# RWKV attention beside a mixture of experts: from tile 10 on a round takes two tiles

## The chip, the core and the metric

The kernel runs on one core of a Trainium2 chip. The time is in microseconds (us) of the device, from one execution of the whole program; the median of three runs is used. The engines are TensorE (PE; its weight loads have a row of their own, PEld), VectorE (DVE), ScalarE (ACT), GpSimd (POOL) and SyncE (SP, which only issues transfers). In the code they are `T`, `V`, `S_`, `G` and `Q`.

## The reference

Attention is a linear recurrence over 768 steps for 4 batches of 8 heads of 48 columns; its output, 3072 tokens of 384 columns, goes through 8 experts whose weights come from a gate that is normalized in turn over rows and columns.

```python
for t in range(S):
    cur = einsum('bhd,bhe->bhde', u[None] * kt, vt)
    y[:, :, t] = einsum('bhd,bhde->bhe', rt, state + cur)
    state = w[None, :, :, None] * state + einsum('bhd,bhe->bhde', kt, vt)
...
logits = x @ w_gate
P = exp(logits - logits.max())
for _ in range(8):
    P /= P.sum(1, keepdims=True) + 1e-09
    P /= P.sum(0, keepdims=True) + 1e-09
    P *= N / E
for e in range(E):
    out += P[:, e:e + 1] * (maximum(x @ w1[e], 0.0) @ w2[e])
```

## The kernel before

**Tiles.** The tokens are 24 tiles of 128 (`NTT`), six to a batch. Attention is done tile by tile in a chunked form. For tile `tt`: `prep_k` (VectorE) scales k into `kp`; r is loaded turned by blocks (`load_blocks`), transposed in blocks by `turn_r` (VectorE, into `rp`) and scaled by `scale_r` (GpSimd, into `rT`); `stage_b` turns k on TensorE (`pkT`) and ScalarE copies it to `kT`; `stage_c` makes the scores (`pA`, 32 matmuls of 64 rows and 64 columns), which VectorE copies through a mask into `at`; `state` makes k's products with v (`pu`), to which VectorE adds the state so far and which GpSimd multiplies by the decay (`sd`); `spread` (ScalarE) lays the state out as `S` for the next tile; `stage_d` sums y in PSUM (`py`: 16 matmuls with `S`, 32 with `at`); `bonus_dot` and `bonus` make the term of u (`rk`, `dg`; GpSimd and VectorE), and `finish` (VectorE) adds it: x. `sum_x`, `scale_x` and `low_x` split x into two half-precision parts (`xsc`) and issue the DMA that transposes it into `hbx`; `stage_f` multiplies it by the gate's weights (`px`) and ScalarE copies the result to `lparts`. A tile whose number is 5, 11, 17 or 23 needs no `state`.

**Units.** Meanwhile expert 0 is computed for groups of three tiles. A unit is a piece of it on TensorE: g1 (`ph`, 9 matmuls, then a relu on ScalarE and the low half `hb` on VectorE) or g2 (`po`, 12 matmuls, then ScalarE copies it to `stg` and SyncE stores it). Units stand in a list, 8 g1 and 3 g2 for the first group, then g1 g2 g1 g2 g1 g2 g1 over and over; `work(n)` takes the next n. Units left over run after the attention.

**Side steps.** Three lists of steps prepare token combinations for the later experts: rebuilds on VectorE (`ws<-hbx`), 17 additions on GpSimd (`ws<-ws`), casts on ScalarE and low parts on VectorE (both `xv`). A cast comes three steps after the last addition that it reads. `prepare()` takes one step, if the tiles that its list needs are there.

**Order.** Every instruction goes to its engine's queue in the order in which the code makes it (`InOrder`), each engine executes its queue in that order, and semaphores between engines follow from the data. So the order of the calls in a round is the order of all queues. Buffers go round: `ps1` has two banks for `ph`, `ps2` two for `po` and `px`, `ps3` four for everything of the attention, and the loaded tiles of k and r three each, of v five. Rounds 0 to 9 and 25, 26 are `open_round`; rounds 10 to 24 are `packed_round(i)`: one unit, two units, `prepare` two or three times, the gate product of tile i - 4, the turn of k of tile i + 1, the scores of i, y of i - 1, the state of i, `prepare` twice. The helper that keeps the order records all instructions under one line, L30, so the profile is read by the names of tiles.

After the attention the gate is normalized and the other seven experts run until the end; the change does not touch that part.

Of the kernel before, what the change touches and what calls it, by code (L numbers as in the profile page):

```python
# [8 lines left out]
F32 = mybir.dt.float32  # L9
# [24 lines left out]
def rwkv_sinkhorn_moe(  # L34
# [37 lines left out]
    TX0 = 12  # L72
    PACKED = 10
    GX = 4
    NWP = 4
# [313 lines left out]
    ss_ = [ac.tile([P, NPAIR, 2, D], F32, name=f"S{i}") for i in range(2)]  # L389
    sd_ = [ac.tile([P, NPAIR, D], F32, name=f"sd{i}") for i in range(2)]  # L390
    for t_ in rp_[:1] + kp_[:1] + rp_[1:] + kp_[1:]:
# [84 lines left out]
    def scale_r(tt):  # L476
        rT = at2.tile([P, NPAIR, P], F32, tag="rT", name=f"rT_{tt}", bufs=3)
        G.tensor_tensor(rT, rp_[tt % 2].rearrange("p (a j) d -> p a (j d)", j=2), tab, op=ALU.mult)
        st.setdefault(tt, {})["rT"] = rT
# [7 lines left out]
    def prep_k(tt):  # L487
        V.tensor_tensor(kp_[tt % 3][:, :, :D], loads[tt]["k"], kt4, op=ALU.mult)

# [35 lines left out]
    def stage_b(tt):  # L525
        d = st.setdefault(tt, {})
        for nm, src in (("rT", rp_[tt % 2]), ("kT", kp_[tt % 3]))[tt >= TX0 :]:
            pt = ps3.tile([P, NPAIR, P], F32, tag="pa", name=f"p{nm}_{tt}")
            sv = src.rearrange("p (a j) d -> p a (j d)", j=2)
            for p_ in range(NPAIR):  # L530
                T.transpose(pt[:, p_, :], sv[:, p_, :], ident)
            dst = at2.tile([P, NPAIR, P], F32, tag=nm, name=f"{nm}_{tt}", bufs=3 if nm == "rT" else 2)
            S_.copy(dst, pt)
            d[nm] = dst
# [23 lines left out]
    def state(tt):  # L558
        c = tt % NCHB
        if c < NCHB - 1:  # L560
            vn = loads[tt]["v"]
            kp = kp_[tt % 3].rearrange("p (a j) d -> p a (j d)", j=2)

            pu = ps3.tile([P, NPAIR, D], F32, tag="pa", name=f"pu_{tt}")
            for p_ in range(NPAIR):
                for j in range(2):
                    T.matmul(
                        pu[j * HP : (j + 1) * HP, p_, :], kp[:, p_, j * HP : (j + 1) * HP],
                        vn[:, 2 * p_ + j, :], start=True, stop=True,
                    )  # L570
            sd = sd_[tt % 2]
            if c == 0:
                V.tensor_tensor(sd, pu, wcb, op=ALU.mult)
            else:
                V.tensor_tensor(sd, pu, sd_[(tt - 1) % 2], op=ALU.add)
                G.tensor_tensor(sd, sd, wcb, op=ALU.mult)

    def spread(tt):
        if tt % NCHB < NCHB - 1:
            sn = ss_[tt % 2]  # L580
            for j in range(2):
                rows = slice(j * HP, (j + 1) * HP)
                S_.copy(sn[rows, :, j, :], sd_[tt % 2][rows])
            st.setdefault(tt + 1, {})["S"] = sn
# [223 lines left out]
    dot_u(0)  # L808
    def packed_round(i):
        if i + 2 < NTT:  # L810
            load_round(i)
        if TX0 <= i + 1 < NTT:
            scale_r(i + 1)
        if i + 2 < NTT:
            prep_k(i + 2)
        if i + 1 < NTT:
            bonus_dot(i + 1)
        if i < NTT:
            bonus(i)
        sum_x(i - 2)  # L820
        if i < NTT:
            spread(i - 1)
        held[0] = True
        work(1)
        held[0] = False
        scale_x(i - 2)
        emitted[0] = i - 1
        form_lows()
        if i + 2 < NTT:
            turn_r(i + 2)  # L830
        low_x(i - 2)
        work(2)
        for _ in range(n_steps(i, 1)):
            prepare()
        stage_f(i - 4, ps2.tile([P, TB], F32, tag="po", name=f"px_{i}"))
        if i + 1 < NTT:
            stage_b(i + 1)
        if i < NTT:
            stage_c(i, lambda: None)
        stage_d(i - 1)  # L840
        finish(i - 1)
        if i < NTT:
            state(i)
        for _ in range(n_steps(i, 2)):
            prepare()
        if i + 4 < NTT:
            load_blocks(i + 4)

# [89 lines left out]

    for i in range(NTT + 3):
        if PACKED <= i <= NTT:  # L940
            packed_round(i)
        else:
            open_round(i)
        if i == NTT + 2:
            stage_f(i - 3, ps2.tile([P, TB], F32, tag="po", name=f"px_{i + 1}"))
        done = i - 2
        if 0 <= done < NTT and done % TH == TH - 1:
            po_ = done // TH
            if po_ == 0:
                units += [g1_unit(0, fc, W) for fc in range(FC)]  # L950
                units += [g2_half(0, t, 0, W) for t in range(TH)]
                pend = [(0, t, 1) for t in range(TH)]
            for j in range(2 if po_ else 0):
                g1 = [g1_unit(po_, fc, W) for fc in range(j * FHC, (j + 1) * FHC)]
                g2 = [g2_half(*a, W) for a in pend]
                units += merged(g1, g2)
                pend = [(po_, t, j) for t in range(TH)]
    assert not side and not wsteps
# [565 lines left out]
```

## Time and profile before

| | |
|---|---|
| median of 3 runs | 1510.43 us (1509.54 to 1510.84) |
| profiled execution | 1511.74 us, of which the span from first to last instruction is 1510.2 us |
| granted clock of TensorE | 1.00 |
| busy over the span | PE 99%, DVE 66%, ACT 46%, POOL 37% |
| rounds 10 to 26 | about 76 to 217 us of the span |

Busy time of an engine is the union of its instructions. A matmul row's duration contains the way through the array, so that successive matmuls overlap: the cost of a group on TensorE is the distance from its start to the start of the next group. The name in `out<-in` says which tile an instruction writes and reads, with buffer numbers left out. What stands in square brackets is the engine's idle time just ahead of the row and what ended it; "issue" means that nothing in the profile was waited for.

### The profile page before, as it was taken

Reading aid. Unit: us, or ns where it says so; the run is one execution under the profiler, and the core shown is the slowest. Engines: PE = TensorE matmul, PEld = TensorE weight load, DVE = VectorE, ACT = ScalarE, POOL = GpSimd, SP = SyncE. Lnnn points to the kernel's source line nnn. Section 1 sums busy time; section 2 is a strip of 40 time slices with the busy share of each in tenths; the row PEclk is TensorE's granted clock in tenths of the full one; section 3 lists DMA queues with packets and bytes.
Section 4 is the critical chain, followed back from the end, with each engine's and each line's share of the span. In section 5 each row is a group of like instructions: output and inputs, shape, how many; then the busy total and the mean of one; then the engine's idle time right before and its main releaser. Section 6 shows DMA issues by size and latency. Waiting matters only on the chain.

```text
span 1510.2 us, 26058 instructions
## 1 busy us (share of the span) xinstructions
PE 1498.7 (99%) x10228; PEld 848.4 (56%) x10228; DVE 1002.8 (66%) x1647; ACT 693.8 (46%) x1289; POOL 562.8 (37%) x667
## 2 busy tenths in 40 slices
PE   8999999999999999999999999999999999999998
PEld 6777766555555555555555555555555555555555
DVE  7888859575666666666666666656566666666563
ACT  7644545244443544445454544445353544445320
POOL 8677845200124243342425243342424233242200
PEclk9999999999999999999999999999999999999999
DMA  9777541212155566766666566655454455555433
GB/s 189 160 175 164 125 112 55 79 47 95 62 105 75 76 126 89 130 80 124 93 108 100 84 126 93 116 61 96 60 100 54 60 95 61 95 62 98 57 97 129
DMA packets 193639, 147.70 MB, mean 98 GB/s; under 512 B 110306, under 2 KB 187748, under 8 KB 193508
## 3 DMA queue, kind: packets, MB, share of 16 engines
q0 software_dynamic: 44928, 61.36, 33.0%
q1 hardware_dynamic: 148370, 84.60, 20.9%
q8 instruction: 82, 1.34, 0.4%
q14 instruction: 49, 0.40, 0.1%
q10 hardware_dynamic: 210, 0.00, 0.0%
HBM read 59.92 MB, written 80.23 MB: 93 GB/s over the span
## 4 chain that ended last, share of the span: by engine, by line
PE 96%; DVE 3%; DMA 0%; issue 0%; ACT 0%; DVEq 0%; ACTq 0%
PE po L30 49%; PE bZ L30 12%; PE bY L30 12%; PE ph L30 5%; PE bA L30 5%; PE bB L30 5%; PE py L30 3%; PE bC L30 2%; PE pA L30 1%; PE pkT L30 1%; PE pu L30 1%; DVE hb L30 0%; DMA hbx<-xsc 0%; DVE wms L30 0%; DVE xv L30 0%
## 5 line engine op out<-in xcount | busy, mean ns | idle before, releaser
L30 PE MATMUL po<-ws,hbx 128*128 128x384 f16 x3360 | 736.8, 326 | 0.0
L30 POOL DMA_DIRECT2D accd<-stg x288 | 249.8, 867 | 695.7 <-ACT stg L30 671.4
L30 PEld LDWEIGHTS <-hbx 128*128 128x128 f16 x3504 | 335.3, 98 | 294.2 <-issue 0.6
L30 PEld LDWEIGHTS <-ws 128*128 128x128 f16 x3096 | 301.7, 98 | 247.5 <-issue 2.0
L30 ACT ACTIVATE hbx<-tb 128x512 f16<-128x512 f32 x224 | 141.1, 630 | 450.5 <-DVE tb L30 450.5
L30 PE MATMUL po<-ws,hb 128*128 128x384 f16 x1248 | 323.1, 326 | 0.0
L30 DVE TENSOR_TENSOR tb<-bY,tb 128x512 f32<-128x512 f32 x168 | 116.2, 691 | 195.3 <-PE bY L30 195.2
L30 ACT ACTIVATE stg<-po,pe 128x384 f32<-128x384 f32 x312 | 179.2, 574 | 121.2 <-PE po L30 93.2
L30 PE MATMUL bZ<-xv,ws 128*128 128x512 f16 x840 | 227.0, 379 | 0.9 <-DVE tb L30 0.9
L30 PE MATMUL bY<-xv,ws 128*128 128x512 f16 x840 | 227.0, 379 | 0.0
L30 DVE TENSOR_TENSOR tb<-bZ,tb 128x512 f32<-128x512 f32 x168 | 115.5, 688 | 134.8 <-PE bZ L30 134.6
L30 PEld LDWEIGHTS <-hb 128*128 128x128 f16 x1248 | 121.4, 98 | 93.9 <-issue 0.2
L30 POOL TENSOR_TENSOR ucb<-rawb 128x256 f32<-128x256 f32 x84 | 75.5, 950 | 117.2 <-DMA rawb<-in_moe_w_dram 117.2
L30 DVE TENSOR_TENSOR tb<-bB,tb 128x512 f32<-128x512 f32 x112 | 77.4, 691 | 49.1 <-PE bB L30 47.2
L30 PE MATMUL ph<-hbx,ws 128*128 128x384 f16 x576 | 103.9, 326 | 2.3 <-DMA hbx<-xsc 1.4
L30 DVE SCALAR_TENSOR_TENSOR hb<-tb,hbx 128x512 f16<-128x512 f32 x112 | 77.2, 689 | 24.6 <-ACT hbx L30 19.5
L30 PE MATMUL bA<-xv,ws 128*128 128x512 f16 x336 | 90.8, 379 | 0.0
L30 PE MATMUL bB<-xv,ws 128*128 128x512 f16 x336 | 90.8, 379 | 0.0
L30 DVE SCALAR_TENSOR_TENSOR hbx<-tb,hbx 128x512 f16<-128x512 f32 x112 | 77.8, 695 | 14.7 <-ACT hbx L30 10.4
L30 ACT COPY tb<-bZ 128x512 f32<-128x512 f32 x56 | 32.7, 585 | 65.6 <-PE bZ L30 65.5
L30 DVE SCALAR_TENSOR_TENSOR hb<-ph,hb 128x384 f16<-128x384 f32 x64 | 35.1, 550 | 26.0 <-ACT hb L30 25.8
L30 DVE TENSOR_REDUCE wms<-rawb 128x1 f32<-128x768 f32 x56 | 51.8, 944 | 0.0
(177 smaller groups left out, 1464.8 us busy)
## 6 DMA issues: line engine op xcount, KB each, us to landing
accd<-stg POOLq DMA_DIRECT2D x288, 192.0 KB, 3.6
rawb<-in_moe_w_dram SPq DMA_DIRECT2D x28, 768.0 KB, 7.3
e0d<-stg SPq DMA_DIRECT2D x48, 192.0 KB, 2.1
hb<-e0d SPq DMA_DIRECT2D x48, 192.0 KB, 3.6
vn<-in_v_dram SPq DMA_DIRECT2D x24, 192.0 KB, 3.3
hbx<-in_r_dram SPq DMA_DIRECT2D x48, 96.0 KB, 2.5
accd<-stg SPq DMA_DIRECT2D x24, 192.0 KB, 1.8
accd<-hb POOLq DMA_DIRECT2D x24, 192.0 KB, 4.8
```

The costliest lines, as they stand in the source:

```text
L30: return lambda *a, **k: self.tc.keep_in_program_order(f(*a, **k))
```

## The change

From tile 10 on a new `double_round(a)` takes tiles a and a + 1. It first runs five or six units, each with some vector work between: the splits of x of the two tiles whose y came last, the scaling of k and r of the new tiles, side steps, and behind the fourth or fifth unit the gate products of the two tiles before those, one after the other. Then come, on TensorE: turns of k of both tiles, state's products of both, y of the two tiles before, scores of both. At its end four more side steps. Nine double rounds and a short end replace rounds 10 to 26. The gate's two tiles, r's homes (`rhome`, four in turn, one of them a part of `kp`), k's (`khome`, two in turn) and the decayed state's (three) are named by hand; loads of k, r and v from tile 14 on are issued in the double round.

```diff
@@ -71,6 +71,7 @@
     NSUM = 4
     TX0 = 12
     PACKED = 10
+    NFIRST = PACKED + 4
     GX = 4
     NWP = 4
 
@@ -387,7 +388,16 @@
     at_ = [ac.tile([P, H, C], F32, name=f"at{i}") for i in range(2)]
 
     ss_ = [ac.tile([P, NPAIR, 2, D], F32, name=f"S{i}") for i in range(2)]
-    sd_ = [ac.tile([P, NPAIR, D], F32, name=f"sd{i}") for i in range(2)]
+    sd_ = [ac.tile([P, NPAIR, D], F32, name=f"sd{i}") for i in range(3)]
+    rt_ = [ac.tile([P, NPAIR, P], F32, name=f"rT{i}") for i in range(3)]
+    rt_.append(kp_[2].rearrange("p (a j) d -> p a (j d)", j=2))
+
+    def rhome(tt):
+        return rt_[tt % 3] if tt < TX0 else rt_[(0, 3, 1, 2)[(tt - TX0) % 4]]
+
+    def khome(tt):
+        return kp_[tt % 3] if tt < TX0 else kp_[tt % 2]
+
     for t_ in rp_[:1] + kp_[:1] + rp_[1:] + kp_[1:]:
         G.memset(t_[:, :, D:], 0.0)
     fill(at_[0].rearrange("p h c -> p (h c)"))
@@ -474,7 +484,7 @@
         V.transpose(rp_[tt % 2].rearrange("p (a j) (q g) -> p a g (j q)", j=2, g=GX), x_)
 
     def scale_r(tt):
-        rT = at2.tile([P, NPAIR, P], F32, tag="rT", name=f"rT_{tt}", bufs=3)
+        rT = rhome(tt)
         G.tensor_tensor(rT, rp_[tt % 2].rearrange("p (a j) d -> p a (j d)", j=2), tab, op=ALU.mult)
         st.setdefault(tt, {})["rT"] = rT
 
@@ -485,7 +495,7 @@
         G.tensor_tensor(rp_[tt % 2][:, :, :D], loads[tt]["r"], rt4, op=ALU.mult)
 
     def prep_k(tt):
-        V.tensor_tensor(kp_[tt % 3][:, :, :D], loads[tt]["k"], kt4, op=ALU.mult)
+        V.tensor_tensor(khome(tt)[:, :, :D], loads[tt]["k"], kt4, op=ALU.mult)
 
     def prep_first():
         for j, (nm, dst) in enumerate((("r", rp_[0]), ("k", kp_[0]))):
@@ -524,12 +534,12 @@
 
     def stage_b(tt):
         d = st.setdefault(tt, {})
-        for nm, src in (("rT", rp_[tt % 2]), ("kT", kp_[tt % 3]))[tt >= TX0 :]:
+        for nm, src in (("rT", rp_[tt % 2]), ("kT", khome(tt)))[tt >= TX0 :]:
             pt = ps3.tile([P, NPAIR, P], F32, tag="pa", name=f"p{nm}_{tt}")
             sv = src.rearrange("p (a j) d -> p a (j d)", j=2)
             for p_ in range(NPAIR):
                 T.transpose(pt[:, p_, :], sv[:, p_, :], ident)
-            dst = at2.tile([P, NPAIR, P], F32, tag=nm, name=f"{nm}_{tt}", bufs=3 if nm == "rT" else 2)
+            dst = rhome(tt) if nm == "rT" else at2.tile([P, NPAIR, P], F32, tag=nm, name=f"{nm}_{tt}")
             S_.copy(dst, pt)
             d[nm] = dst
 
@@ -559,7 +569,7 @@
         c = tt % NCHB
         if c < NCHB - 1:
             vn = loads[tt]["v"]
-            kp = kp_[tt % 3].rearrange("p (a j) d -> p a (j d)", j=2)
+            kp = khome(tt).rearrange("p (a j) d -> p a (j d)", j=2)
 
             pu = ps3.tile([P, NPAIR, D], F32, tag="pa", name=f"pu_{tt}")
             for p_ in range(NPAIR):
@@ -568,11 +578,11 @@
                         pu[j * HP : (j + 1) * HP, p_, :], kp[:, p_, j * HP : (j + 1) * HP],
                         vn[:, 2 * p_ + j, :], start=True, stop=True,
                     )
-            sd = sd_[tt % 2]
+            sd = sd_[tt % 3]
             if c == 0:
                 V.tensor_tensor(sd, pu, wcb, op=ALU.mult)
             else:
-                V.tensor_tensor(sd, pu, sd_[(tt - 1) % 2], op=ALU.add)
+                V.tensor_tensor(sd, pu, sd_[(tt - 1) % 3], op=ALU.add)
                 G.tensor_tensor(sd, sd, wcb, op=ALU.mult)
 
     def spread(tt):
@@ -580,7 +590,7 @@
             sn = ss_[tt % 2]
             for j in range(2):
                 rows = slice(j * HP, (j + 1) * HP)
-                S_.copy(sn[rows, :, j, :], sd_[tt % 2][rows])
+                S_.copy(sn[rows, :, j, :], sd_[tt % 3][rows])
             st.setdefault(tt + 1, {})["S"] = sn
 
     def stage_d(tt):
@@ -806,45 +816,89 @@
     prep_r(2)
     spread_u()
     dot_u(0)
-    def packed_round(i):
-        if i + 2 < NTT:
-            load_round(i)
-        if TX0 <= i + 1 < NTT:
-            scale_r(i + 1)
-        if i + 2 < NTT:
-            prep_k(i + 2)
-        if i + 1 < NTT:
-            bonus_dot(i + 1)
-        if i < NTT:
-            bonus(i)
-        sum_x(i - 2)
-        if i < NTT:
-            spread(i - 1)
-        held[0] = True
+    def px_bank(tt):
+        return ps2.tile([P, TB], F32, tag="po", name=f"px_{tt}")
+
+    KR = {"k": k, "r": r, "v": v}
+    unscaled, turned_x = [], []
+
+    def double_round(a):
+        b = a + 1
+        first, inside = a == PACKED, a < NTT
+
+        def load(tt, nms):
+            for nm in nms if NFIRST <= tt < NTT else "":
+                load_part(tt, nm, KR[nm])
+
+        load(a + 2, "kr")
+        load(b, "v")
+        if first:
+            stage_b(b)
+            spread(a - 1)
+            sum_x(a - 2)
+        if a - first <= NTT:
+            bonus(a - (not first))
+        if inside and not first:
+            scale_r(a)
         work(1)
-        held[0] = False
-        scale_x(i - 2)
-        emitted[0] = i - 1
-        form_lows()
-        if i + 2 < NTT:
-            turn_r(i + 2)
-        low_x(i - 2)
-        work(2)
-        for _ in range(n_steps(i, 1)):
+        ready = turned_x[:]
+        turned_x.clear()
+        for tt in unscaled:
+            scale_x(tt)
+            work(1)
+            low_x(tt)
+            emitted[0] = tt + 1
+            turned_x.append(tt)
+        unscaled.clear()
+        if inside and not first:
+            prep_k(a)
+            bonus_dot(a)
+            prep_k(b)
+            scale_r(b)
+        work(1)
+        for _ in range(4):
             prepare()
-        stage_f(i - 4, ps2.tile([P, TB], F32, tag="po", name=f"px_{i}"))
-        if i + 1 < NTT:
-            stage_b(i + 1)
-        if i < NTT:
-            stage_c(i, lambda: None)
-        stage_d(i - 1)
-        finish(i - 1)
-        if i < NTT:
-            state(i)
-        for _ in range(n_steps(i, 2)):
+        work(1)
+        for tt in ready:
+            stage_f(tt, px_bank(tt))
+        if inside and not first:
+            bonus(a)
+        work(1 if inside else 0)
+        prepare()
+        load(a + 3, "kr")
+        load(a + 2, "v")
+        if a > NTT:
+            return
+        if inside and not first:
+            stage_b(a)
+            stage_b(b)
+        if inside:
+            state(a)
+            if a + 2 < NTT:
+                turn_r(a + 2)
+            state(b)
+        for n, tt in enumerate((a - 2, a - 1)):
+            if tt < PACKED - 1:
+                continue
+            stage_d(tt)
+            if inside and not (first and n):
+                spread(a - 1 + n)
+            finish(tt)
+            if inside and n and b + 2 < NTT:
+                turn_r(b + 2)
+            sum_x(tt)
+            unscaled.append(tt)
+        if first:
+            spread(a)
+        if inside:
+            bonus_dot(b)
+            stage_c(a, lambda: None)
+            stage_c(b, lambda: None)
+        for tt in (a + 4, b + 4):
+            if tt < NTT:
+                load_blocks(tt)
+        for _ in range(4):
             prepare()
-        if i + 4 < NTT:
-            load_blocks(i + 4)
 
     def open_round(i):
         if i == 1:
@@ -936,25 +990,35 @@
             finish(i - 1)
             planned(i, "d")
 
-    for i in range(NTT + 3):
-        if PACKED <= i <= NTT:
-            packed_round(i)
-        else:
-            open_round(i)
-        if i == NTT + 2:
-            stage_f(i - 3, ps2.tile([P, TB], F32, tag="po", name=f"px_{i + 1}"))
-        done = i - 2
-        if 0 <= done < NTT and done % TH == TH - 1:
-            po_ = done // TH
+    grouped = [0]
+
+    def more_units(done):
+        while grouped[0] < done // TH:
+            po_ = grouped[0]
+            grouped[0] += 1
             if po_ == 0:
-                units += [g1_unit(0, fc, W) for fc in range(FC)]
-                units += [g2_half(0, t, 0, W) for t in range(TH)]
-                pend = [(0, t, 1) for t in range(TH)]
+                units.extend(g1_unit(0, fc, W) for fc in range(FC))
+                units.extend(g2_half(0, t, 0, W) for t in range(TH))
+                pend[:] = [(0, t, 1) for t in range(TH)]
             for j in range(2 if po_ else 0):
                 g1 = [g1_unit(po_, fc, W) for fc in range(j * FHC, (j + 1) * FHC)]
                 g2 = [g2_half(*a, W) for a in pend]
-                units += merged(g1, g2)
-                pend = [(po_, t, j) for t in range(TH)]
+                units.extend(merged(g1, g2))
+                pend[:] = [(po_, t, j) for t in range(TH)]
+
+    for i in range(PACKED):
+        open_round(i)
+        more_units(i - 1)
+    unscaled.append(PACKED - 2)
+    turned_x.extend((PACKED - 4, PACKED - 3))
+    for a in range(PACKED, NTT + 3, 2):
+        double_round(a)
+        more_units(emitted[0])
+    work(3)
+    for tt in turned_x:
+        stage_f(tt, px_bank(tt))
+    while side:
+        side.pop(0)()
     assert not side and not wsteps
     att.close()
 
```

## The prediction

> **What bounds the kernel now.** I read the page's busy table and chain first, then the waits, then TensorE's timeline from 74 us on, then the durations of the attention rounds by tile. These lines of the page carry the bound:
>
> ```profile
> span 1510.2 us, 26058 instructions
> ...
> PE 1498.7 (99%) x10228; PEld 848.4 (56%) x10228; DVE 1002.8 (66%) x1647; ACT 693.8 (46%) x1289; POOL 562.8 (37%) x667
> ...
> PE   8999999999999999999999999999999999999998
> ...
> PE 96%; DVE 3%; DMA 0%; issue 0%; ACT 0%; DVEq 0%; ACTq 0%
> ```
>
> TensorE (PE) issues without a break for 99% of the span and is 96% of the chain that ended last. So only two things can move the time: how long PE's own stream takes, and idle time put into it. The change rewrites rounds 10 to 26, about 76 to 217 us; the same matmuls run before and after. The table of busy time by stretch shows eleven of these rounds (tiles 12 to 22 in their steady order):
>
> ```profile
> core 0: us, PE busy (x) PEld busy (x) DVE busy (x) ACT busy (x) POOL busy (x), PEclk, DMA share, GB/s
> ...
> 94.51:191.39 96.88, 96.88 (x1461) 70.61 (x1458) 84.96 (x151) 47.35 (x113) 82.23 (x83) 1.00 0.68 152
> ```
>
> PE is busy for all 96.88 us, 8.81 a round, at full clock. But VectorE (DVE) is busy 88% and GpSimd (POOL) 85%: the order of before hides two nearly full engines. That is the cover I have to test.
>
> **Part 1: fewer changes of matmul form.** TensorE's timeline of one round and pieces of others (start, length, matmul group):
>
> ```profile
> 81.11 0.64 PE L30 MATMUL prT<-ident,rp 128*128 128x128 f32 x4
> 81.58 0.60 PE L30 MATMUL pkT<-ident,kp 128*128 128x128 f32 x4
> ...
> 93.49 1.09 PE L30 MATMUL py<-vn,at 128*64 128x48 f32 x32
> 94.51 3.10 PE L30 MATMUL ph<-hbx,ws 128*128 128x384 f16 x18
> 97.45 2.11 PE L30 MATMUL po<-ws,hb 128*128 128x384 f16 x12
> 99.40 0.29 PE L30 MATMUL px<-wgp,hbx 128*128 128x16 f16 x6
> 99.55 0.64 PE L30 MATMUL pkT<-ident,kp 128*128 128x128 f32 x4
> 100.12 1.10 PE L30 MATMUL pA<-rT,kT 64*64 64x128 f32 x32
> 101.15 0.88 PE L30 MATMUL py<-S,rT 128*64 128x96 f32 x16
> 101.86 1.09 PE L30 MATMUL py<-vn,at 128*64 128x48 f32 x32
> 102.78 0.64 PE L30 MATMUL pu<-vn,kp 128*64 128x48 f32 x16
> 103.35 1.64 PE L30 MATMUL ph<-hbx,ws 128*128 128x384 f16 x9
> ```
> The weight loads of the same round, with PE's own idle time ahead of them:
> ```profile
> 100.12 0.86 PEld L30 LDWEIGHTS pA<-rT,kT 64*64 64x64 f32 x32 [0.17 <-issue]
> 101.15 0.69 PEld L30 LDWEIGHTS py<-S,rT 128*64 128x64 f32 x16 [0.17 <-issue]
> ```
> From start to next start: four turns of k followed by another form take 0.57 (99.55 to 100.12), four turns followed by the same form 0.47 (81.11 to 81.58), so that end costs 0.10, and the idle rows give 0.17 for each of k to scores and scores to y. y followed by units takes 1.02 (93.49 to 94.51), y followed by state's products of the same form 0.92: 0.10 for the way back to the units. Into the turns of k I allow 0.04. A round so pays 0.04 + 0.17 + 0.17 + 0.10 = 0.48, two rounds 0.96. The change orders two tiles as turns k, k; state, state; y, y; scores, scores. That has one entry (0.04), turns to state, y to scores, and one exit (0.10). The two middle neighbours stand in no row of before; the nearest rows are the two of 0.17, so I take 0.17 each: 0.48 for two tiles. Seven pairs (tiles 10 to 23) save 7 x 0.48 = 3.4 us. If the new neighbours cost nothing it is 5.7, if twice as much 1.0.
>
> The one wait of PE in these rounds also goes, since round 10 no longer turns r and k of tile 11 ahead of y of tile 9:
>
> ```profile
> 83.46 0.88 PE L30 MATMUL py<-S,rT 128*64 128x96 f32 x16 [0.25 <-ACT rT L30]
> ```
> That is 0.25. Next in line there is PE itself. Parts that only rename homes (`rhome`, `khome`, the third `sd`) add no instruction and cost nothing: they cover nothing.
>
> **Part 2: two gate products in a row.** In these rounds gate products (px) and g2 units (po) share the two banks of `ps2`. Before, each round has one px; after, px of two tiles stand back to back. The trace of before has this once, at its end:
>
> ```profile
> 216.50 0.29 PE L30 MATMUL px<-wgp,hbx 128*128 128x16 f16 x6
> 216.75 0.48 ACT L30 COPY stg<-po 128x384 f32<-128x384 f32 x1 [1.50 <-PE po L30]
> 217.12 0.28 ACT L30 ACTIVATE lparts<-px,inv_s 128x16 f32<-128x16 f32 x1
> 217.28 0.29 PE L30 MATMUL px<-wgp,hbx 128*128 128x16 f16 x6 [0.48 <-ACT stg L30]
> ```
> The second px needs the bank of the g2 unit just ahead, which ScalarE (ACT) has still to copy out: 217.28 - 216.50 = 0.78 instead of 0.16, so 0.62. Where a g1 unit stands ahead and a g2 unit behind, that g2 unit waits instead for `lparts` of the first px, behind the unit's own relu: about as long. The units come in sevens, g1 g2 g1 g2 g1 g2 g1; 11 are used when round 10 begins. Counting on with 5, 5, 6, 6, 6, 6, 6, 5, 5 units a double round, g2 stands ahead of a px pair in the double rounds of tiles 10, 18 and 22, and behind one in that of tile 20 and after the last: 5 x 0.57 = 2.8 us new (0 if ScalarE's copy were early each time, 3.1 at 0.62 each). The pair at the very end waits as before.
>
> **Part 3: the queues of VectorE, GpSimd and ScalarE.** They execute in the order written. Durations (shortest/median/longest ns) of the attention rounds:
>
> ```profile
> L30 POOL TENSOR_TENSOR rT<-rp,hb x12: 1267/1277/1984, 88.8 to 184.3; 128x512 f32<-128x512 f32 x12
> L30 POOL TENSOR_TENSOR rk<-rn,kn x12: 988/1006/1383, 90.0 to 186.3; 128x384 f32<-128x384 f32 x12
> L30 POOL TENSOR_TENSOR rk<-rk,ub x12: 997/1008/1200, 91.4 to 187.3; 128x384 f32<-128x384 f32 x12
> L30 POOL TENSOR_TENSOR rk<-vn,dg x13: 817/832/1551, 92.4 to 194.0; 128x384 f32<-128x384 f32 x13
> L30 POOL TENSOR_TENSOR ws<-ws x51: 716/727/1451, 84.7 to 204.4; 128x256 f32<-128x256 f32 x51
> L30 DVE COPY_PREDICATED at<-mask,pA x28: 708/740/757, 84.5 to 198.3; 128x512 f32<-128x512 int32 x28
> L30 DVE TENSOR_TENSOR kp<-kn,ktab x11: 529/579/1617, 86.5 to 174.5; 128x384 f32<-128x384 f32 x11
> L30 DVE SCALAR_TENSOR_TENSOR xsc<-x,xs,xsc x13: 541/1021/1373, 89.4 to 194.6; 128x384 f16<-128x384 f32 x13
> L30 DVE TENSOR_TENSOR xv<-ws,xv x8: 1003/1226/1543, 95.2 to 179.8; 128x768 f16<-128x768 f32 x6, 128x1024 f16<-128x1024 f32 x2
> L30 DVE TENSOR_TENSOR ws<-hbx x6: 942/1116/1346, 130.6 to 188.1; 128x768 f32<-128x768 f16 x6
> L30 DVE TENSOR_REDUCE dg<-rk x13: 532/540/553, 86.9 to 191.9; 128x8 f32<-128x384 f32 x13
> L30 DVE SCALAR_TENSOR_TENSOR hb<-ph,hb x22: 539/545/558, 90.4 to 197.0; 128x384 f16<-128x384 f32 x22
> L30 ACT COPY kT<-pkT x12: 584/586/596, 91.9 to 188.3; 128x512 f32<-128x512 f32 x12
> L30 ACT CAST xv<-ws x8: 823/836/1048, 92.3 to 178.7; 128x768 f16<-128x768 f32 x6, 128x1024 f16<-128x1024 f32 x2
> L30 ACT ACTIVATE hb<-ph x22: 470/490/494, 89.3 to 196.5; 128x384 f16<-128x384 f32 x22
> ```
> VectorE instructions with two inputs in SBUF (kp, xsc) spread from 0.53 to 1.6, those that read PSUM or one input (dg, hb, at) stay within 7%; GpSimd's spread too. The two engines hold each other up. I bound every wait from both sides: nobody held up, and held up as in the long rows.
>
> *Tiles 12 and 13* (clock from the first unit). VectorE does four copies at (3.0), one xv (1.0) and dg of tile 11 (0.5) before GpSimd can form rk<-vn,dg: 4.5. GpSimd then runs that (0.8), rT (1.3), rk twice (2.0), rT (1.3), and the add on which ScalarE's next cast depends (0.7): 10.6. ScalarE stands in that cast, and behind it are stg 0.48, lparts 0.28, hb 0.49 and kT 0.59: with the cast's 0.84 it is 13.3. PE has done three g1 (1.47 each: 94.51 to 97.45 for two), two g2 (1.95: 97.45 to 99.40), a px (0.16), two turns (0.94) and two states (1.2): 10.6. Its y of tile 10 needs the bank that kT leaves: 2.6 late, or 1.3 where queued instructions overlap and nobody is held up. Before, a turned k had a whole round until its scores.
>
> *Tiles 16 and 17.* VectorE must do four at, two rebuilds (ws<-hbx), dg, two hb, two xsc, two kp ahead of k's second turn: 3.0 + 1.9 + 0.5 + 1.1 + 1.1 + 1.1 = 8.6 at the shortest, and six one-column instructions. PE asks for it after four g1, two g2, two px and one turn: 10.6. Nothing held up, it is in time; with xsc and kp at their long ends (up to 0.83 and 1.09 more each) it is 1.5 late, and the lateness runs on into the banks that `sd` and x free: 3.1 in all, 1.2 without hold-ups.
>
> *Tiles 14 and 15, 20 and 21.* hb stands behind two kp: 0 to 1.1. In 20 and 21 an xv, three rebuilds, an hb and a dg (1.0 + 2.8 + 1.1 = 4.9) come between kp and `sd`, whose bank the scores need; PE has about 4.8 there, and the turn of r lies in between: 0.6 to 2.0. Two more waits of 0.3 are among the long ends. Sum: 3.1 with nobody held up (1.3 + 1.2 + 0.6), 9.1 held up (2.9 + 1.1 + 3.1 + 2.0). The rows lie on both ends (medians of kp near the short, of xsc near the middle), so I take the middle: 6.1.
>
> The Trainium skill bears on this end: "SBUF — State Buffer", section "SBUF: two separate sides", says the port pair that VectorE and GpSimd share is an exclusive lock, whose loser waits for the whole instruction. By that rule the sum of this part would be 9.1 rather than 6.1; the spread of kp up to 1.6 agrees with it.
>
> The change adds one wait by itself: `sd` of the second tile now follows GpSimd's product on `sd` of the first within the same double round. On VectorE both x and the second turn of r are queued behind it, and PE's scores wait for their banks; it is inside the 2.0 and 3.1 above.
>
> SyncE: loads stand at the head and behind the sixth unit, a double round ahead of use, the transposing DMAs right behind each xsc as before, `load_blocks` at the end behind both turns of r. What waits there (a slot of k, freed by GpSimd) has stores of stg behind it, of which three may be open. I give this nothing, since the same queue held loads that waited for GpSimd in every round of before; a loss here belongs to the upper end.
>
> **Sum.** -3.4 - 0.25 + 2.8 + 6.1 = +5.3. The profiled execution took 1511.74 us (span 1510.2 and 1.5 around it), 1.3 above the median 1510.43 of the timed runs; it becomes 1517.0, a median of 1515.7.
>
> **Rivals.** *Faster: the slack is enough* and ScalarE's copies come before the second px: only part 1 and the lost wait stay, -3.65, 1506.8. It decides if kT and kp always come before PE's 10.6. For it: no PE wait in eleven rounds. Against: the row at 217.28 and 88% of VectorE. *No change: parts 1 and 2 alone*, -0.85, 1509.6: as above but the pairs of px wait. *Slower still: full hold-ups*, -3.65 + 2.8 + 9.1 = +8.3, 1518.7; new neighbours at their dear end add 2.4. This is also what the rule quoted above gives.
>
> **How the numbers follow.** A change under 0.2%, 3.0 us, can't be told from none. Forecast (1513.4 to 1517.2): 0.40; full hold-ups or more: 0.25; no change (1507.4 to 1513.4): 0.25; faster: 0.10. So faster 0.10, same 0.25, slower 0.65. The range 1508.5 to 1521.5 leaves about 1 in 10 on each side: below, part 3 gone and the pairs half hidden; above, full hold-ups with dear neighbours. The forecast's own range is 1513.4 to 1517.2.
>
> **What will show it.** Right: between 76 and 217 us half the 0.17 idle rows; PE waits on ACT stg at px pairs; PE waits at y of tile 10 for ACT kT, at k's second turn of 17 for DVE kp, at the scores of 16, 17 and 20 for DVE sd or x; ScalarE casts that wait for GpSimd. Wrong: TensorE's rows without waits from 86 to 217 us, or a wait on SyncE's loads, or new forms that cost more than 0.17.

## The result, and the profile after

After takes 1521.22 us, the median of six runs (1520.21 to 1524.53), against 1510.91 for before on the same chip (six runs, 1509.54 to 1514.37): the ratio is 1.0070, 95% interval 1.0055 to 1.0085, that is +8 to +13 us, +10.3 at the medians. A second time, on another chip, it came out at 1.0072 (1.0055 to 1.0089). The prediction had 1515.7, with 1508.5 to 1521.5 as its range: slower, as forecast, but by twice as much, and at the very edge of the range: the median of the second time, 1522.30, lies outside it.

The page of after, its span, busy line and chain by engine (of before: 1510.2 us, PE 1498.7, chain PE 96%):

```profile
span 1519.1 us, 26042 instructions
PE 1501.2 (99%) x10228; PEld 850.7 (56%) x10228; DVE 1001.0 (66%) x1647; ACT 693.1 (46%) x1289; POOL 558.0 (37%) x667
PE 83%; DVE 2%; ACT 0%; issue 0%; ACTq 0%; DVEq 0%
```

TensorE's busy time and count hardly moved, so the time is idle time, or time in which it ran slowly. What a whole run took is a blunt measure here: r's turn of tile 10, ahead of which the kernels run the same program, starts between 63.6 and 68.2 us in the profiled executions of this study. I therefore measure one stretch inside each trace: from r's turn of tile 10 to the first product of the next stage (`bA`). Its two rows in TensorE's timeline of before, then of after (start, length, group):

```profile
65.42 0.64 PE L30 MATMUL prT<-ident,rp 128*128 128x128 f32 x4
...
282.17 0.81 PE L30 MATMUL bA<-xv,ws 128*128 128x512 f16 x3
```
```profile
63.56 0.64 PE L30 MATMUL prT<-ident,rp 128*128 128x128 f32 x4
...
292.10 0.81 PE L30 MATMUL bA<-xv,ws 128*128 128x512 f16 x3
```

282.17 - 65.42 = 216.75 before, 292.10 - 63.56 = 228.54 after: +11.8. The second execution of after gives 228.58, and the kernel `gaps` below, which is before up to this point, gives 216.77, so the stretch repeats within 0.1. (The profiled spans differ by only 8.9: after's began its stretch 1.9 us earlier and took 1.0 less behind it.)

The waits view of after, 75 to 232 us, TensorE's entries and one of ScalarE's (us in all, times, longest). Before had one of 0.25 for ACT rT in these rounds and the pair of px at the end:

```profile
ACT xv L30 <- POOL ws L30: 9.8, 3, 5.0
...
PE py L30 <- ACT kT L30: 2.5, 2, 2.3
PE px L30 <- ACT stg L30: 1.9, 4, 0.5
PE pA L30 <- DVE sd L30: 1.7, 1, 1.7
PE pkT L30 <- DVE kp L30: 1.1, 2, 0.9
PE po L30 <- ACT lparts L30: 0.9, 2, 0.5
...
PE po L30 <- DVE hb L30: 0.6, 1, 0.6
...
PE pA L30 <- DVE x L30: 0.4, 1, 0.4
```

And where they lie, in TensorE's timeline of after (the bracket is its idle time and what ended it): y of tile 10, a g2 unit of tiles 14/15, k's turn of 17, the scores of 17 and of 20:

```profile
101.48 1.55 PE L30 MATMUL py<-S,rT 128*64 128x96 f32 x16 [2.35 <-ACT kT L30]
102.81 1.90 PE L30 MATMUL py<-vn,at 128*64 128x48 f32 x32
...
119.26 0.34 PE L30 MATMUL po<-ws,hb 128*128 128x384 f16 x1 [0.63 <-DVE hb L30]
...
138.03 0.66 PE L30 MATMUL pkT<-ident,kp 128*128 128x128 f32 x4 [0.89 <-DVE kp L30]
...
144.45 1.46 PE L30 MATMUL pA<-kp,kT 64*64 64x128 f32 x32 [0.44 <-DVE x L30]
...
182.05 0.98 PE L30 MATMUL pA<-rT,kT 64*64 64x128 f32 x26 [1.70 <-DVE sd L30]
```

One thing in them was not forecast. Behind the first wait y's 16 products last 1.55 us instead of 0.88 and its next 32 last 1.90 instead of 1.09. The table of busy time by stretch (PEclk is the third column from the right) says why:

```profile
101.50:104.50 3.00, 3.00 (x48) 3.00 (x50) 2.88 (x5) 0.42 (x1) 2.01 (x2) 0.50 1.02 211
...
182.10:184.60 2.50, 2.50 (x60) 2.14 (x60) 2.50 (x5) 1.82 (x6) 2.38 (x3) 0.74 0.11 23
184.60:187.00 2.40, 2.40 (x11) 1.20 (x10) 2.22 (x4) 0.00 (x0) 2.32 (x5) 0.56 0.00 0
```

Behind the two longest waits TensorE ran at about half its clock. Lost: 3.0 x 0.50 + 2.5 x 0.26 + 2.4 x 0.44 = 3.2 us, which no column of idle time shows.

### The profile page after: what moved, and what is told of

The parts are those of the page before. It is cut to its first block, busy times and chain, and to the rows that moved or that the text cites. A ratio compares the mean times of both kernels' runs of the same rounds, so it can differ in the third digit from the quotient of the medians.

```text
span 1519.1 us, 26042 instructions
## 1 busy us (share of the span) xinstructions
PE 1501.2 (99%) x10228; PEld 850.7 (56%) x10228; DVE 1001.0 (66%) x1647; ACT 693.1 (46%) x1289; POOL 558.0 (37%) x667
## 4 chain that ended last, share of the span: by engine, by line
PE 83%; DVE 2%; ACT 0%; issue 0%; ACTq 0%; DVEq 0%
PE po L30 46%; PE bZ L30 12%; PE bY L30 12%; PE bA L30 5%; PE bB L30 5%; PE bC L30 2%; PE ph L30 2%; DVE xv L30 0%; DVE wms L30 0%; DVE tb L30 0%; DVE hb L30 0%; DVE rs_s L30 0%; DVE pm L30 0%; DVE cs_s L30 0%; ACT hbx L30 0%
```

## The experiments

My theory: the loss is part 3, the queues of VectorE, GpSimd and ScalarE, at the upper end of its bounds because the two engines hold each other up, with the loss of clock on top. The rivals: the new order of TensorE's own stream costs the time; or the order of the queues alone does, with no hold-ups; or idle time and clock have nothing to do with each other.

| kernel | stretch, us | median, us | ratio to before, 95% interval |
|---|---|---|---|
| before | 216.75 | 1510.91 | |
| after | 228.54, again 228.58 | 1521.22, again 1522.30 | 1.0070 (1.0055 to 1.0085), again 1.0072 (1.0055 to 1.0089) |
| n_before | 216.17 | 1511.16 | 0.9995 (0.9985 to 1.0004) |
| n_after | 216.17 | 1512.14 | 0.9996 (0.9987 to 1.0005) |
| n_px_k | 213.32 | 1507.41 | 0.9975 (0.9966 to 0.9984) |
| fill | 226.09 | 1519.90 | 1.0053 (1.0039 to 1.0066) |
| px_apart | 226.38 | 1519.95 | 1.0052 (1.0038 to 1.0066) |
| one12 | 224.54 | 1519.17 | 1.0050 (1.0036 to 1.0065) |
| no_hold | 222.65 | 1517.85 | 1.0036 (1.0021 to 1.0050) |
| u_best | 217.36 | 1511.40 | 1.0002 (0.9993 to 1.0011) |
| c_best | 215.46 | 1510.59 | 0.9991 (0.9982 to 1.0000) |

The kernels were timed on several chips, each beside before on the same chip; there before's medians were 1510.91 (after), 1512.63 (n_before, n_after, fill, px_apart), 1512.30 (n_px_k, one12, u_best, c_best) and 1511.61 (no_hold and after again). So ratios can be compared, medians of different chips only roughly. A stretch is that of one profiled execution.

**Is it the queues? The token preparation left out, in after and in before.** The steps that `prepare` takes from `side` are the work that the two orders place differently among the attention's:

```diff
-        side += steps
+        side += [] if sg < 3 else steps
```

> The kernel after, without its token preparation in the rounds (three groups of three rebuilds on VectorE, 17 sums on GpSimd, four casts on ScalarE and four differences on VectorE; two groups have the casts, the third has not): that part of the computation is left out and the home of its results is set to zero behind the last round. Theory (the queues of VectorE, GpSimd and ScalarE are late because these steps stand among the attention's): the waits of TensorE for ACT kT (2.35), DVE hb (0.79 at 118 us), DVE kp (1.16) and DVE sd (1.70) go, and with the two long ones the stretches of half clock; what is left of the change is part 1 and 2, -3.3 - 0.3 + 3.1, so the kernel is -2 to +1.5 us against the order of before without the same steps. Rival (the new order of TensorE's own stream, or its loads on SyncE, costs the time): it stays +7 to +11 us above it.

> The kernel before, without the same token preparation (left out, its home set to zero behind the last round). Theory and rival alike: no wait of TensorE goes, since there is hardly one, so its rounds are within 1 us of before; it is the base for the kernel after without that preparation. If instead it is 5 us or more faster than before, the preparation costs TensorE time in the order of before too, by a way that its trace does not show.

Both stretches are 216.17 us: the order of after costs nothing on balance once those steps are gone. The waits view of the kernel after without them, 70 to 240 us, has only the pairs of px left:

```profile
PE px L30 <- ACT stg L30: 1.9, 4, 0.5
PE po L30 <- ACT lparts L30: 0.9, 2, 0.5
```

So the first rival falls, and SyncE's moved loads with it: they are all still there. What the steps cost is 228.54 - 216.17 = 12.4 us in the order of after and 216.75 - 216.17 = 0.6 in that of before.

**What is part 1 worth, and part 2?** The same kernel, with the two gate products apart and k scaled early, so that no wait is left in its rounds:

```diff
         turned_x.clear()
+        if len(ready) > 1:
+            stage_f(ready[0], px_bank(ready.pop(0)))
...
-        for tt in ready:
-            stage_f(tt, px_bank(tt))
         if inside and not first:
             bonus(a)
         work(1 if inside else 0)
+        for tt in ready:
+            stage_f(tt, px_bank(tt))
...
-            prep_k(a)
             bonus_dot(a)
-            prep_k(b)
...
             stage_c(b, lambda: None)
+            for tt in (a + 2, b + 2):
+                if tt < NTT:
+                    prep_k(tt)
```

> The kernel after without the token preparation in its rounds (left out, as in n_after), with the gate products apart and both tiles' k scaled at the end of the double round before. Theory: no wait is left, so part 1 shows alone: 3.3 + 0.3 us less than n_before between r's turn of tile 10 and the first product of the next stage (216.17 there), that is 212.6 to 213.5, and -2 to -3.5 us as a whole. Rival (the new neighbours of matmul forms cost as much as the old): 215.5 to 216.5.

213.32, inside the expectation: fewer changes of form save 216.17 - 213.32 = 2.85 against n_before, and the pairs of px cost the same 2.85 (n_after against this). The whole run is 0.25% faster than before, of which the missing preparation is 0.05% (n_before): the rest is what the order could give if everything else kept up. One sign named ahead can be read here too: of the idle rows of 0.17 in TensorE's weight loads, n_before has 25 in the rounds and n_px_k 13, half as forecast. Of the two places that the sum named, turns to state has its rows; the others lie at scores to units, and y to scores has none.

**The pairs of px in the full kernel.** After, with the same edit of `stage_f` alone:

> The kernel after, with the two gate products of a double round apart: the first behind the first unit, the second behind the sixth. Theory (each pair costs one wait of 0.60 to 0.62 us for a bank, in five double rounds): -1.5 to -3.1 us against after, 1518.1 to 1519.7, the lower gain if TensorE, now earlier, waits longer at kT, kp and sd. Rival (these waits lie beside waits for the other engines' queues, which only come later): within 0.5 us of after. In the trace the rows of px with 0.47 to 0.48 behind ACT stg are gone from 82, 154, 194 us and those of po behind lparts at 172 and 223 too.

The waits for stg and lparts are gone but for the one at the very end, and the stretch is 2.2 us shorter: as expected, less than the 2.85 because the wait for `sd` grew by 0.5.

**The clock.** After, with more TensorE work inside its two long waits:

```diff
-            state(b)
+            state(b, {12: 5, 20: 4}.get(a, 1))
```
(`state` issues its products so many times over.)

> The kernel after, with the state's products of tile 13 issued five times and those of tile 21 four times (the same result, over the same bank), which puts about 1.9 and 1.4 us more of TensorE work into its waits of 2.35 (ACT kT) and 1.70 us (DVE sd). Theory (standing idle for about 2 us is what halves the clock for some 3 us behind it): the stretch behind the first wait (101.48 to 104.50 at clock 0.50) and that behind the second (184.64 to 187.00 at 0.57) run at full clock, which gives 3.0 x 0.50 = 1.5 and 2.4 x 0.43 = 1.0: about 2.5 us faster than the kernel after, 1518.7, although TensorE does 3.3 us more work. Rival (the low clock has another cause, or other engines set the end of these rounds): no gain, 1521 to 1522, up to 3 us slower if the products push the queues further.

The same three stretches in this kernel; the waits ahead of them are 0.48 and 0.3 now:

```profile
101.50:104.50 3.00, 2.52 (x74) 2.45 (x72) 2.94 (x4) 0.99 (x3) 2.59 (x3) 1.00 0.50 126
182.10:184.60 2.50, 2.50 (x59) 1.87 (x52) 2.50 (x4) 1.82 (x6) 2.42 (x4) 1.00 0.06 10
184.60:187.00 2.40, 2.40 (x16) 1.44 (x15) 2.37 (x7) 0.49 (x1) 2.32 (x4) 1.00 0.00 0
```

TensorE does 3.3 us more work, and the stretch is 2.4 us shorter: full clock throughout. It is not the 3.2 of the rows because the wait for hb at 118 us grew from 0.63 to 1.15, and a wait of 0.24 lies ahead of the change, at 66 us. At these two places idle time is what lowers the clock.

**One step's place.** After, with the four steps behind the fourth unit moved behind the state's products, in the double round of tiles 12 and 13 alone:

> The kernel after with one thing moved: in the double round of tiles 12 and 13 the four steps of the token preparation behind the fourth unit (one difference on VectorE, GpSimd's sums, the cast on ScalarE) stand behind the state's products instead. Theory (ScalarE stands in the cast for GpSimd, 5.03 us, and the copy of k's turn stands behind it): TensorE's wait of 2.35 at y of tile 10 goes, with the 1.5 of half clock behind it: -3.9 at the place. The steps now meet the same queues later, so hb of the next double round (0.79 before) grows to 2 or 3, and what the whole gains is only -0.5 to -2.5: 1518.7 to 1520.7. Rival (the lateness at y of tile 10 comes from the attention's own work: four copies, products of r and k): the wait stays over 1.5 there.

The wait at y of tile 10 is gone, and with it the slow stretch behind it; the lateness did turn up at hb of the next double round, but at 1.77 us instead of 0.63. The stretch is 4.0 shorter, while the median, 1519.17, is within what I expected of the whole. That 4.0 looks like the 3.9 expected at the place, but it is made up otherwise: about 4.1 at y of tile 10, less some 1.6 in the next double round, and 1.6 more at the scores of tile 20. For there the wait for `sd` is as long as in after, yet the clock behind it stays full (timeline, then the stretch table):

```profile
118.33 0.34 PE L30 MATMUL po<-ws,hb 128*128 128x384 f16 x1 [1.77 <-DVE hb L30]
...
181.72 0.98 PE L30 MATMUL pA<-rT,kT 64*64 64x128 f32 x26 [1.70 <-DVE sd L30]
```
```profile
182.00:184.00 2.00, 2.00 (x62) 1.65 (x55) 2.00 (x4) 1.74 (x6) 1.92 (x3) 1.00 0.11 23
184.00:186.00 2.00, 2.00 (x15) 1.21 (x13) 2.00 (x5) 0.58 (x2) 2.00 (x4) 1.00 0.00 0
```

So the length of a wait does not settle it; the second run of after and a kernel with 36 waits put into it, both below, follow that up.

**Hold-ups or order?** In after, kp lasts twice as long as before (durations: shortest/median/longest ns), and the timeline shows it end just behind an instruction of GpSimd, which is itself stretched:

```profile
L30 DVE TENSOR_TENSOR kp<-kn,ktab x12: 545/1217/1625, 94.7 to 194.5; 128x384 f32<-128x384 f32 x12
```
```profile
134.73 1.29 POOL L30 TENSOR_TENSOR rk<-rk,ub 128x384 f32<-128x384 f32 x1
135.08 2.90 DVE L30 TENSOR_TENSOR kp<-kn,ktab 128x384 f32<-128x384 f32 x2
135.98 1.58 POOL L30 TENSOR_TENSOR kp<-rp,hb 128x512 f32<-128x512 f32 x1
```

The two kp end at 135.08 + 2.90 = 137.98, 0.42 behind the end of rT (whose home is called kp here), 137.56. The test keeps GpSimd's queue as long and takes its large operands away (`out[s]` is eight columns):

```diff
-        G.tensor_tensor(rk, ld_["r"], ld_["k"], op=ALU.mult)
+        g_op(rk, ld_["r"], ld_["k"], ALU.mult, 1005)
...
+        G.tensor_tensor(out[s], a_[s], b_[s], op=op)
+        left = ns - 200
+        while left > 100:
+            m = min(n - 8, max(8, int((left - 98) / 0.833)))
+            G.memset(flat_[:, 8 : 8 + m], 0.01)
+            left -= 98 + 0.833 * m
```

> The kernel after, in whose double rounds GpSimd does each product and sum over eight columns only and fills the rest of the same home with a constant, in fills of the same length together (1.27, 1.00, 0.83, 0.73, 0.59 us): that part of the computation is left out. GpSimd's queue is as long and in the same order, but its instructions no longer read two large operands beside VectorE's. Theory (VectorE and GpSimd hold each other up, which is why part 3 came out at its upper end: kp has a median of 1.22 in after, 0.58 before): kp falls to 0.55, TensorE's waits at kp, hb and sd go or fall under 0.7, kT to about 1.3, and the half clock goes: 219 to 222 us from r's turn of tile 10 to the first product of the next stage (228.53 after, 216.75 before), -6 to -9 us as a whole. Rival (the order of the queues alone): 226 to 229, within 2 us of after.

Durations in this kernel, then its wait for kT and the clock behind it:

```profile
L30 DVE TENSOR_TENSOR kp<-kn,ktab x12: 545/552/576, 98.5 to 191.6; 128x384 f32<-128x384 f32 x12
...
L30 DVE SCALAR_TENSOR_TENSOR xsc<-x,xs,xsc x11: 607/618/653, 97.9 to 190.6; 128x384 f16<-128x384 f32 x11
```
```profile
104.58 1.26 PE L30 MATMUL py<-S,rT 128*64 128x96 f32 x16 [1.64 <-ACT kT L30]
```
```profile
104.30:108.00 3.70, 3.42 (x58) 3.43 (x60) 3.10 (x6) 0.71 (x2) 2.20 (x10) 0.58 0.95 203
```

Every kp and xsc is at its short end, the rounds' waits at kp and hb are gone, and the stretch is 5.9 us shorter. That is half of the loss: the hold-ups are real, and with them gone the order of the queues still costs 222.65 - 216.17 = 6.5, of which 1.6 is clock. The expectation was 219 to 222 and missed by 0.7, because the wait for kT is still 1.64 and still takes the clock to 0.58; the whole run gained only 4.5 of the expected 6 to 9. The Trainium skill, "SBUF — State Buffer", section "SBUF: two separate sides", has the port pair of VectorE and GpSimd as a lock held for a whole instruction, which a VectorE instruction with two inputs in SBUF meets only against a GpSimd instruction that reads SBUF; both traces agree (median of kp 1.22 in after, 0.55 in this kernel, where fills took the place of the products).

**What gap costs clock?** Before, with idle time put into its later stages, where TensorE is otherwise dense:

```diff
+                    if 2 <= s <= 4 and i % 5 == 4:
+                        gap((8, 160, 320, 480, 640)[gaps[0] % 5])
```
(`gap` makes a small product wait for a copy on ScalarE and a sum of so many columns on GpSimd.)

> The kernel before with idle time of TensorE put into its later stages: 36 times a small product waits for a chain over ScalarE and GpSimd of five lengths (about 1.1, 1.4, 1.8, 2.1, 2.4 us and more where those engines are busy). Nothing of the computation is left out. Theory (idle time of some 1.7 us can halve the clock behind it, depending on where it falls; 1.2 us can't): the products of 512 columns behind the gaps, 0.21 us apart at full clock, are 0.43 apart for about 3 us behind some of the longer gaps and behind none of the short ones. Rival: the clock is lost only behind idle time of about 3.4 us, as the Trainium skill has it in "TensorE: Matmul & The Clock Gate"; then no gap under 3 us has such rows.

The queues made the gaps longer than planned, 1.9 to 5.2 us, so nothing under 1.9 was tried. Behind idle time up to 1.9 us no clock was lost (0 of 2), behind 2.1 to 2.7 in 6 of 12, behind 2.9 to 3.2 in 7 of 11, behind 3.5 and more in 11 of 11; the slow stretch lasts 2.6 to 5.8 us. Two gaps of one length, in the timeline and in the stretch table behind them:

```profile
655.08 0.39 PE L30 MATMUL pz<-gs,ident 128*128 128x8 f32 x2 [2.14 <-POOL gs L30]
...
845.04 0.60 PE L30 MATMUL pz<-gs,ident 128*128 128x8 f32 x2 [2.14 <-POOL gs L30]
```
```profile
655.10:659.00 3.90, 3.90 (x22) 2.17 (x23) 1.26 (x2) 0.58 (x1) 0.00 (x0) 1.00 0.46 50
845.10:849.00 3.90, 3.90 (x13) 1.89 (x14) 0.00 (x0) 0.59 (x1) 0.00 (x0) 0.57 0.38 48
```

The rival of 3.4 us falls, and so does any fixed length: where the gap falls may count too, as the two of 2.14 suggest. The second run of after was to show the same of the attention rounds:

> The kernel after once more, on the same chip as the two others: 1519.5 to 1522. If the clock behind a wait depends on where the wait falls and not on its length alone, the wait of 1.70 for sd may be without the stretch of half clock this time; the longer wait of 2.35 has it again.

There both waits lost the clock again (2.36 at kT; the one at `sd`, and the clock behind it, are these rows):

```profile
183.12 0.98 PE L30 MATMUL pA<-rT,kT 64*64 64x128 f32 x26 [1.74 <-DVE sd L30]
```
```profile
185.60:188.00 2.40, 2.40 (x12) 1.06 (x9) 2.29 (x5) 0.00 (x0) 2.32 (x5) 0.57 0.00 0
```

Of the four executions with an `sd` wait of 1.70 to 1.74, three lost it (after twice, px_apart) and one12 did not.

**A better order.** Two versions, one pattern for all double rounds and one chosen for each; their common edit replaces the fixed calls of `prepare`, `stage_f` and `prep_k` by places in a table:

```diff
         work(1)
-        for _ in range(4):
-            prepare()
+        for m in range(n + 1, 5):
+            gates(m)
+        slot(4)
         work(1)
-        for tt in ready:
-            stage_f(tt, px_bank(tt))
+        gates(5)
```

> The order of after with its waits taken apart: the gate products behind the first and the sixth unit; the even tile's k scaled at the end of the double round before; the token preparation, eight steps a double round instead of nine, as one behind the second low part of x, four behind the fourth unit, one behind the sixth, two behind the state's products (after: four behind the fourth unit, one behind the sixth, four at the end). Theory: the px waits (3.1) and the clock loss (2.5) go and most of the 6 to 7 us of queue waits: -8 to -11 against after, 1510 to 1513, so within 0.2% of before. Rival (any place for these steps costs as much, because VectorE and GpSimd are full): only the px waits go, -2 to -3, 1518 to 1519.

> As the one before, but with the steps of the token preparation, the places of the gate products and of k's scaling chosen for each double round apart. Theory (what is left is a matter of which queue is late in which double round): waits of TensorE in the rounds under 2 us in all, 1508.5 to 1511.5, between 2.4 us faster than before and the same. Rival: VectorE's and GpSimd's work itself is longer than TensorE's, and waits of 5 us or more stay wherever the steps stand: 1514 or more.

u_best wins back 11.2 of the 11.8 us and is as fast as before (1.0002). c_best's stretch is 1.3 us shorter than that of before, and its ratio is 0.9991 (0.9982 to 1.0000): level with before or a trifle faster, some 0.1%, and well ahead of after. Its waits in TensorE, 70 to 300 us, the first of which lies behind the rounds:

```profile
PE po L30 <- DVE hb L30: 1.1, 1, 1.1
PE ph L30 <- DVE hb L30: 0.6, 1, 0.6
PE px L30 <- ACT stg L30: 0.5, 1, 0.5
```

VectorE and GpSimd have the same work as in after: only the places of the steps, of the gate products and of k's scaling differ. So "any place costs as much" falls too. In the new places kp is held up less, too: its median, 1.22 in after, is 0.62 in u_best and 0.70 in c_best.

## Why the prediction was right, and where its size was off

| step | forecast, us | measured, us | from |
|---|---|---|---|
| part 1, fewer changes of form | -3.4 (-5.7 to -1.0) | -2.85 | n_px_k against n_before |
| the lost wait of rT | -0.25 | its row is gone (inside the 0.6 that n_before is below before) | waits of after, n_before |
| part 2, pairs of px | +2.8 | +2.85 | n_after against n_px_k |
| part 3, queues | +6.1 (3.1 to 9.1) | +11.8, of it 3.2 clock | after less before, each less its kernel without the steps |
| sum | +5.3 | +11.8 in the stretch, +10.3 in the medians | |

**Right.** The direction, parts 1 and 2, and every place but one (the scores of 16 show no wait): the px pairs wait in the double rounds of tiles 10, 18 and 22 for stg, and behind the pairs of 20 and the last a g2 unit waits for lparts; y of tile 10 waits for kT, a unit of 14/15 for hb, k's second turn of 17 for kp, the scores of 17 for x and of 20 for `sd`; ScalarE's casts wait for GpSimd (5.0 the longest). TensorE waited for none of SyncE's loads; the waits view puts one wait down to a load, 1.0 us of GpSimd ahead of an `sd`. The step for tiles 12 and 13 came out as a sum. The double round's first unit and the queues of GpSimd and ScalarE in after:

```profile
88.58 2.12 PE L30 MATMUL po<-ws,hb 128*128 128x384 f16 x12
...
92.28 0.82 POOL L30 TENSOR_TENSOR rk<-vn,dg 128x384 f32<-128x384 f32 x1
...
93.07 1.26 POOL L30 TENSOR_TENSOR rT<-rp,hb 128x512 f32<-128x512 f32 x1
...
96.87 1.59 POOL L30 TENSOR_TENSOR kp<-rp,hb 128x512 f32<-128x512 f32 x1
...
98.42 2.90 POOL L30 TENSOR_TENSOR ws<-ws 128x256 f32<-128x256 f32 x4
99.19 0.83 ACT L30 CAST xv<-ws 128x768 f16<-128x768 f32 x1 [5.03 <-POOL ws L30]
...
100.83 1.08 ACT L30 COPY kT<-pkT 128x512 f32<-128x512 f32 x2
```

The cast starts 10.6 behind the unit, as forecast for the add that it needs. Part of that is luck: GpSimd began its products 0.8 us earlier than worked out (3.7 behind the unit instead of 4.5) and took 0.8 longer for them, held up. The first kT is out at about 101.4, 12.8 behind it (forecast 13.3), while TensorE was ready at 101.48 - 2.35 = 99.13, 10.55 behind it (forecast 10.6).

**Mis-sized: part 3.** "The rows lie on both ends (medians of kp near the short, of xsc near the middle), so I take the middle: 6.1." That step failed. The medians were read from before, but the change itself moves kp beside GpSimd's products and sums: its median went from 0.58 to 1.22, nine of the twelve above 1 us. Without the clock part 3 is 11.8 - 3.2 = 8.6, near the upper bound of 9.1, and without hold-ups the whole loss halves (no_hold). The row nearest to the new case was not the median of all kp before but the long kp, those that began while a product or sum of GpSimd was running. Place by place, as the lateness that each adds against n_after from start to start of the same groups, the clock's share (3.2 in after, 1.6 in no_hold) taken out:

| place | forecast, us | after | no_hold |
|---|---|---|---|
| y of tile 10 | 1.3 to 2.6 | 2.5 | 1.8 |
| a unit of 14/15 | 0 to 1.1 | 0.8 | 0 |
| tiles 16 and 17 | 1.2 to 3.1 | 3.2 | 1.7 |
| the scores of 20 | 0.6 to 2.0 | 2.2 | 0.9 |

So after lies at the dear end almost everywhere, and the cheap end was itself too low: with nobody held up the places cost 4.4, not 3.1. (The upper bound of 9.1 has 2.9 for the first place, where its working gives 2.6.)

**Missing: the clock.** The sum priced a wait at its length. Two of the waits cost 3.2 us more than that, which is why the time lies above even the rival "slower still" (1518.7), whose condition, full hold-ups, was met in most places.

**Luck.** That the median is inside the range, by 0.3 us, is luck. The range's upper end stood for full hold-ups with dear new neighbours; the neighbours came out cheap enough to save 2.85, and what filled the range to its edge was the clock, which the prediction did not have.

**The rivals.** "No change: parts 1 and 2 alone" is what n_after measures, and their balance is zero there. "Faster" comes nearest to n_px_k. Both need what this kernel lacks, idle time on VectorE and GpSimd at the right moments.

## What to carry to other kernels

When work of a full engine is moved, bound its instructions by what it will stand beside after the move, not by their median before: two engines that hold each other up keep the order of their queues but change the durations in them. Price a wait of TensorE of about 2 us above its length, since the clock behind it may halve for some 3 us; a few repeated products inside the wait bring that back. And a saving on the bounding engine (2.85 us here) is only collected when the steps on the others are placed again for the new order; c_best, so placed, collected 1.3 of it.

## What the runs showed of the hardware that was not expected

TensorE's clock fell to about half (0.50 to 0.58) behind idle time of 1.64, 1.70 and 2.35 us in the attention rounds, of small products, while in the dense stages neither of two gaps of 1.9 us cost any clock, half of those of 2.1 to 2.7 did, and all from 3.5 us on. The Trainium skill, "TensorE: Matmul & The Clock Gate", section "Part 1: The HAM clock gate", has the clock at full or half only, set by activity in a window of 3.4 us that runs freely. The equal gaps of 2.14 us with different ends agree with a window that does not start with the gap; that it takes about 3 us of idle time to lose the clock, as that page's section "Why this matters for your kernels" has it, does not hold here, where the measurement decides. Whether the attention rounds lose it more easily than the dense stages stays open: 1.70 to 1.74 us was enough in three of four executions there, 1.9 us in neither of two gaps here, which is too few to tell, and how busy the small products keep TensorE is a guess that no run tested.
